# The MLP's last weight, w4, cut into loads in another way

## The chip, the core and the metric

The kernel runs on one core of one Trainium2 chip. The metric is the device time of one execution in microseconds (us), as the median of several runs.

## The reference

One decode step with one token of 512 values. `xn` is the layer norm of `x`. Two branches read it. The first is attention over a cache: 32 heads of 128, and of each head's K and V cache the last 4096 rows are used (32 heads x 4096 x 128 x 2 bytes, 33.5 MB each for K and V). The second is a small MLP with the weights w1 to w4. The result joins the two:

```
q  = xn @ wq                               # 32 heads of 128
s  = softmax(q . k / sqrt(128)) . v @ wo   # last 4096 rows of each head
x1 = xn + hs                               # hs: shifted gelu(ln(xn) @ w1) @ w2; zero for one token
g  = silu(x1 + gelu(ln(x1) @ w3) @ w4)     # w3: 512 x 1376, w4: 1376 x 512
out = x + s * g
```

With one token all four shifted parts of `h` are zeros, so the kernel neither loads w1 nor computes h; it multiplies w2 with zeros.

## The kernel before

The kernel streams K and V once and is otherwise arranged around that stream.

**Loads.** Three small loads go out on ACT: `x_bf`, `x_row` (four rows, one to every 32nd partition) and `wq_sb` (4 MB). All others go out on SP through `load` (L75 to L76): `w2_sb`, `w3_sb`, then w4 in two loads (L91, L92), then the K and V tiles, and the wo rows between and behind them. Ten rows of w4 go to each of 128 partitions (10 KB in one piece: partition p holds rows 10p to 10p+9), and the 96 rows that are left go one to a partition, in the tile's eleventh column. A K or V tile (`load_kv`) is 4 MB for a group of four heads. The first K tile comes in two halves, and so do its computations; the last V tile comes in three pieces. There are three K buffers and two V buffers, so a load waits until the tile that it replaces has been used.

**Order.** In the main part, `tc.manual_schedule` keeps TensorE, VectorE and ScalarE in the order in which the loop over steps `s` writes the work out. Step s loads K of group s and V of group s-2. For each K tile, VectorE computes 64 or 80 of the 128 score columns as products and sums (`k_vector`, L321 and L323); the other columns are transposed on TensorE (`k_turn`, L339), copied by ScalarE (L342) and multiplied with q on TensorE (`k_scores`, L350). The softmax of a group runs a step later, the products with V (`v_wide`, L427) two steps later. V buffers and the last wo rows reuse the memory of the weights (`wts`), so the first V load waits until the MLP is done with them. At the end, `v_part` (L461) uses the last piece of V, `v_out` (L471) divides, `y_head` multiplies the last four heads with wo (L155), and L651 and L653 join the branches and store the result.

**The MLP.** It runs while the stream starts. `a_ps` (L252) takes z3 times w3 as rows: the 1376 values lie in PSUM rows 0, 32, 64 and 96, three blocks of 128 in each. Block i must hold the values that go with the i-th w4 row of every partition, so w3's columns are read with a stride. Gelu (L255), transposes (L258) and a copy (L260) turn them into columns `a_bf`. Then 4 matmuls with w2 and 11 with w4 (L270) add up into `hr_ps`, one for each w4 row of a partition. `hr` (L273) copies the sum, two small steps (L155, L278) bring it into rows, and L280 gives `g_row`, which is used at the very end.

Of the kernel before, what the change touches and what calls it, by code (L numbers as in the profile page):

```python
# [8 lines left out]
P = 128  # L9
BF16 = mybir.dt.bfloat16  # L10
# [16 lines left out]
def kernel(  # L27
# [16 lines left out]
    Bb, Sq, D = A_x.shape  # L44
# [8 lines left out]
    PB = P // G  # L53
    KC = D // P
    F = B_w3.shape[1]
    assert F == 10 * P + 96
    scale = float(Dh) ** -0.5


# [13 lines left out]
    wts = wts_guard.__enter__()  # L73

    def load(dst, src):  # L75
        return tc.keep_in_program_order(nc.sync.dma_start(out=dst, in_=src))  # L76
# [10 lines left out]
    load(w2_sb[:], B_w2.rearrange("(p c) n -> p c n", p=P))  # L87
    w3_sb = wts.tile([P, KC, F], BF16, name="w3_sb")
    load(w3_sb[:], B_w3.rearrange("(p c) n -> p c n", p=P))
    w4_sb = wts.tile([P, 11, D], BF16, name="w4_sb")  # L90
    load(w4_sb[:, 0:10, :], B_w4[0:10 * P, :].rearrange("(p c) n -> p c n", p=P))  # L91
    load(w4_sb[0:96, 10, :], B_w4[10 * P:F, :])  # L92


    def load_kv(pool, cache, g, cuts=(0, CP)):
# [107 lines left out]
    for b in range(2):  # L203
        zeros(qr[b][:])
        for c in range(KC):
            wc = wq_sb[:, c, :].rearrange("p (g a d) -> p g a d", a=G, d=Dh)
# [38 lines left out]
    a_ps = ps_misc.tile([P, 3, P], FP32, tag="misc", name="a_ps")  # L245
    zeros(a_ps[:])
    for c in range(KC):
        wc = w3_sb[:, c, 0:10 * P].rearrange("p (q r) -> p r q", r=10)
        parts = [(j, a_ps[32 * j:32 * j + 1, :, :], wc[:, 3 * j:3 * j + 3, :]) for j in range(3)]
        parts += [(3, a_ps[96:97, 0, :], wc[:, 9, :]), (3, a_ps[96:97, 1, 0:96], w3_sb[:, c, 10 * P:F])]  # L250
        for j, dst, w in parts:
            nc.tensor.matmul(dst, lhsT=z3_bf[:, c:c + 1], rhs=w, start=False, stop=(c == KC - 1),  # L252
                             skip_group_check=True)
# [8 lines left out]
    hr_ps = ps_misc.tile([P, KC, P], FP32, tag="misc", name="hr_ps")  # L262
    zeros(hr_ps[:])
    terms = [(shifted_bf[:, c:c + 1], w2_sb[:, c, :]) for c in range(KC)]
    for i in range(11):
        n = P if i < 10 else 96
        terms.append((a_bf[0:n, i % 3, i // 3:i // 3 + 1], w4_sb[0:n, i, :]))
    for i, (col, w) in enumerate(terms):
        r = 32 * (i % 4)
# [415 lines left out]
```

## Time and profile before

| | before |
|---|---|
| median of 3 runs | 193.7 us (193.29 to 194.14) |
| profiled execution: span | 191.2 us |
| DMA | 79.02 MB, mean 413 GB/s |
| packets | 4572, of these under 2 KB 1232 |
| VectorE busy | 150.9 us (79%) |
| TensorE matmul busy | 116.4 us (61%) |
| ScalarE busy | 89.2 us (47%) |

The span runs from the first to the last instruction of one profiled execution; the timed runs hold some 2.5 us more around it. Busy time is a sum over the whole span. A load's packets are spread over 16 DMA engines. The page gives the engines' mean share; the trace also keeps every packet's start and duration, and, for every load, one increment of its completion semaphore from each DMA engine that took part. A load has landed when the last of them has come.

### The profile page before, as it was taken

The page shows a single profiled execution, that of the slowest core. Times are in us where ns is not written, and L with a number is a line of the kernel's source. Part 1 is how long each engine was busy: PE and PEld are TensorE (multiplying, and loading weights), DVE is VectorE, ACT ScalarE, POOL GpSimd, SP SyncE. Part 2 cuts the span into 40 slices and gives each one's busy share as a digit, 9 for nine tenths or more (in the row PEclk, how much of TensorE's full clock was granted, in tenths as well). Part 3 has the DMA queues.
Part 4 walks back from the last instruction along what each step waited for, and adds up shares of the span by engine and source line. Part 5 has one row for each costly group of instructions (what it writes and reads, how often), then busy time and mean ns, then how long its engine had stood idle before and what let it go on. Part 6 is the DMA issues. An engine that isn't in the chain of part 4 may idle for free.

```text
span 191.2 us, 2839 instructions
## 1 busy us (share of the span) xinstructions
PE 116.4 (61%) x1159; PEld 74.2 (39%) x1159; DVE 150.9 (79%) x175; ACT 89.2 (47%) x191; POOL 2.3 (1%) x11
## 2 busy tenths in 40 slices
PE   1653754989825368256845772680888189739762
PEld 0430222767614334143334441540763077313322
DVE  1660159979999999999999999999999999980111
ACT  2001370888794076427464564542475148733120
POOL 2110000000000000000000000000000000000000
PEclk9999695555755557955695588557567858975998
DMA  6999999999999999999999999999999998999990
GB/s 211 447 430 404 431 418 439 439 439 437 432 434 439 432 429 432 432 439 432 422 432 432 418 422 418 452 439 435 439 432 434 435 432 372 471 425 405 420 371 32
DMA packets 4572, 79.02 MB, mean 413 GB/s; under 512 B 624, under 2 KB 1232, under 8 KB 1488
## 3 DMA queue, kind: packets, MB, share of 16 engines
q1 hardware_dynamic: 4264, 74.65, 91.6%
q10 hardware_dynamic: 296, 4.20, 5.1%
q8 instruction: 9, 0.15, 0.3%
q14 instruction: 3, 0.02, 0.0%
HBM read 78.84 MB, written 0.00 MB: 412 GB/s over the span
## 4 chain that ended last, share of the span: by engine, by line
DVE 46%; DMA 43%; PE 5%; ACT 3%; issue 1%; SPq 1%; ACTq 0%; DVEq 0%
DMA kv<-in_A_k_cache_dram 31%; DVE S L323 28%; DVE prod L321 15%; DMA kv<-in_A_v_cache_dram 10%; ACT kt L342 3%; DMA x_bf<-in_A_x_dram 2%; PE pt L339 2%; PE ov L427 1%; DVE m L366 1%; DVE S L364 1%; SPq L76 1%; PE sT L350 1%; DVE mx L374 1%; PE oT L461 1%; PE ot_ps L444 0%
## 5 line engine op out<-in xcount | busy, mean ns | idle before, releaser
L323 DVE TENSOR_REDUCE S<-prod 128x20 f32<-128x2560 bf16 (+1 forms) x32 | 86.0, 2686 | 1.1
L342 ACT COPY kt<-pt 128x1024 bf16<-128x1024 bf16 x52 | 51.2, 1013 | 40.4 <-PE pt L339 38.7
L339 PE MATMUL pt<-ident_f,kv 128*128 128x128 f32 x208 | 46.7, 376 | 10.8 <-DMA kv<-in_A_k_cache_dram 10.8
L321 DVE TENSOR_TENSOR prod<-kv,q_bc 128x2560 bf16<-128x2560 bf16 (+1 forms) x32 | 45.4, 1418 | 3.9 <-DMA kv<-in_A_k_cache_dram 3.7
L339 PEld LDWEIGHTS pt<-ident_f,kv 128*128 128x128 f32 x208 | 34.2, 196 | 14.4 <-DMA kv<-in_A_k_cache_dram 10.5
L350 PE MATMUL sT<-q_pair,kt 128*128 128x8 bf16 x416 | 19.4, 170 | 15.7 <-ACT kt L342 15.5
L350 PEld LDWEIGHTS <-kt 128*128 128x128 bf16 x416 | 16.4, 104 | 26.8 <-ACT kt L342 25.8
L427 PE MATMUL ov<-kv,pT 128*16 128x512 bf16 x248 | 22.0, 515 | 1.4 <-DMA kv<-in_A_v_cache_dram 1.4
L388 ACT ACTIVATE pT<-S,mb 128x128 bf16<-128x128 f32 x32 | 13.9, 573 | 0.3
L372 PE MATMUL mt_ps<-ident_f,m 128*1 128x128 f32 x8 | 2.9, 359 | 17.4 <-DVE rden L399 16.9
L433 ACT COPY ov_sb<-ov 128x512 f32<-128x512 f32 x8 | 4.7, 586 | 17.1 <-PE ov L427 17.1
L427 PEld LDWEIGHTS <-pT 128*16 128x16 bf16 x248 | 6.9, 109 | 13.2 <-issue 11.4
L359 ACT ACTIVATE own<-sT,par 128x48 f32<-128x48 f32 (+1 forms) x32 | 7.5, 356 | 3.7 <-PE sT L350 3.7
L444 PE MATMUL ot_ps<-ident_f,ov_sb 128*128 128x128 f32 x32 | 7.1, 359 | 2.9 <-ACT mb L384 1.9
L211 DVE CAST q_row<-qr_ps 128x512 bf16<-128x512 f32 x1 | 0.7, 692 | 9.9 <-PE qr_ps L208 9.9
L388 ACT ACTIVATION_READ_ACCUMULATOR pT<-S,mb 128x1 f32 x32 | 8.3, 258 | 0.0
L372 PEld LDWEIGHTS mt_ps<-ident_f,m 128*1 128x1 f32 x8 | 0.6, 80 | 17.9 <-DVE rden L399 17.2
L399 DVE RECIPROCAL rden<-den_ps 128x4 f32<-128x4 f32 x8 | 1.4, 175 | 7.0 <-PE den_ps L394 7.0
L381 PE MATMUL mb_ps<-md,par_t 5*128 5x4 f32 x16 | 3.9, 311 | 4.1 <-DVE md L376 4.1
L255 ACT ACTIVATE a_row<-a_ps 128x384 bf16<-128x384 f32 x1 | 0.5, 491 | 12.0 <-remote 12.0
L444 PEld LDWEIGHTS ot_ps<-ident_f,ov_sb 128*128 128x128 f32 x32 | 4.5, 178 | 3.9 <-ACT mb L384 2.3
L208 PE MATMUL qr_ps<-wq_sb,xq_bf 128*1 128x512 bf16 x32 | 3.1, 566 | 3.7 <-DMA wq_sb<-in_A_wq_dram 3.7
(122 smaller groups left out, 81.6 us busy)
## 6 DMA issues: line engine op xcount, KB each, us to landing
kv<-in_A_k_cache_dram SPq DMA_DIRECT2D x7, 4096.0 KB, 31.3
kv<-in_A_v_cache_dram SPq DMA_DIRECT2D x7, 4096.0 KB, 30.6
wq_sb<-in_A_wq_dram ACTq DMA_DIRECT2D x1, 4096.0 KB, 17.6
kv<-in_A_k_cache_dram SPq DMA_DIRECT2D x2, 2048.0 KB, 27.4
wo<-in_A_wo_dram SPq DMA_DIRECT2D x1, 2048.0 KB
kv<-in_A_v_cache_dram SPq DMA_DIRECT2D x1, 2048.0 KB
kv<-in_A_v_cache_dram SPq DMA_DIRECT2D x2, 1024.0 KB, 17.6
w_sb<-in_B_w_dram SPq DMA_DIRECT2D x1, 1376.0 KB, 9.1
```

The source lines that it names most:

```text
L321: nc.vector.tensor_tensor(out=prod[:, 0:m, :], in0=kn[:, rows, :], in1=q_bc[:, g:g + 1, :].to_broadcast([P, m, Dh]), op=ALU.mult)
L323: nc.vector.tensor_reduce(out=st[g]["S"][:, rows], in_=prod[:, 0:m, :], axis=AX.X, op=ALU.add)
L339: nc.tensor.transpose(pt[:, i, :], kn[:, c:c + 2, :].rearrange("p c d -> p (c d)").bitcast(FP32), ident_f[:])
L342: nc.scalar.copy(out=kts[b][:, 0:n, :], in_=pt[:, 0:n, :].bitcast(BF16))
L350: nc.tensor.matmul(st[g]["sT"][:, c:c + 2, :].rearrange("p c a -> p (c a)"), lhsT=kt[:, i, l::2], rhs=q_pair[:, g, l, :], start=(l == 0), ...
L359: nc.scalar.mul(s["own"][:, 0:m, a], s["sT"][:, 0:m, a], par[:, a:a + 1])
L372: nc.tensor.transpose(mt_ps[:], s["m1"][:], ident_f[:])
L381: nc.tensor.matmul(mb_ps[:], lhsT=par_t[:].rearrange("k b a -> k (b a)"), rhs=md[:], start=True, stop=True)
L388: nc.scalar.activation(out=s["pT"][:, :, a], in_=s["S"][:], func=ACT.Exp, scale=scale, bias=mb[:, a:a + 1], accum_out=s["sum"][:, a:a + 1])
L427: nc.tensor.matmul(ov[r:r + 4 * G], lhsT=s["pT"][:, c:c + 4, :].rearrange("p i a -> p (i a)"), rhs=v[:, c:c + 4, :], start=(i < 4), stop=( ...
L433: nc.scalar.copy(out=s["ov_sb"][:], in_=ov[:])
L444: nc.tensor.transpose(ot_ps[:, step * j:step * j + P], s["ov_sb"][:, j, :], ident_f[:])
```

## The change

w4's 1376 rows are cut as 9 x 128 + 216 + 8 instead of 10 x 128 + 96. Nine rows go to each partition. The next 216 rows are cut into 72 pieces of three rows (3 KB each), which go to 72 partitions in columns 9 to 11; the source is written as six runs of twelve pieces (`e = lanes`). Eight rows of 1 KB go to partitions 72 to 79 in column 9. SP issues three loads for w4 where it issued two. The a_ps matmuls follow: for each of the four c there are three wide ones, three of 72 columns and one of 8, where there were three wide ones, one of 128 and one of 96. hr_ps has 12 products with w4 instead of 11: nine with 128 rows, one with 80 and two with 72. The tile w4_sb has 12 columns instead of 11.

```
-    w4_sb = wts.tile([P, 11, D], BF16, name="w4_sb")
-    load(w4_sb[:, 0:10, :], B_w4[0:10 * P, :].rearrange("(p c) n -> p c n", p=P))
-    load(w4_sb[0:96, 10, :], B_w4[10 * P:F, :])
+    w4_sb = wts.tile([P, 12, D], BF16, name="w4_sb")
+    few, lanes = 72, 6
+    f_few, f_rest = 9 * P, 9 * P + 3 * few
+    load(w4_sb[:, 0:9, :], B_w4[0:f_few, :].rearrange("(p c) n -> p c n", p=P))
+    load(w4_sb[0:few, 9:12, :].rearrange("p c n -> p (c n)"),
+         B_w4[f_few:f_rest, :].rearrange("(i e c) n -> e i (c n)", e=lanes, c=3))
+    load(w4_sb[few:few + F - f_rest, 9, :], B_w4[f_rest:F, :])
...
-        wc = w3_sb[:, c, 0:10 * P].rearrange("p (q r) -> p r q", r=10)
+        wc = w3_sb[:, c, 0:f_few].rearrange("p (q r) -> p r q", r=9)
         parts = [(j, a_ps[32 * j:32 * j + 1, :, :], wc[:, 3 * j:3 * j + 3, :]) for j in range(3)]
-        parts += [(3, a_ps[96:97, 0, :], wc[:, 9, :]), (3, a_ps[96:97, 1, 0:96], w3_sb[:, c, 10 * P:F])]
+        wf = w3_sb[:, c, f_few:f_rest].rearrange("p (i e r) -> p r e i", e=lanes, r=3)
+        parts += [(3, a_ps[96:97, r, 0:few].rearrange("o (e i) -> o e i", e=lanes), wf[:, r]) for r in range(3)]
+        parts += [(3, a_ps[96:97, 0, few:few + F - f_rest], w3_sb[:, c, f_rest:F])]
...
-    for i in range(11):
-        n = P if i < 10 else 96
+    for i in range(12):
+        n = P if i < 9 else few + F - f_rest if i == 9 else few
```

More of the change, by code (lines that the diff above doesn't have):

```diff
@@ L55 @@
     F = B_w3.shape[1]
-    assert F == 10 * P + 96
+    assert F == 9 * P + 3 * 6 * 12 + 8
     scale = float(Dh) ** -0.5
```

## The prediction

> **What bounds the kernel now.** I read the page's DMA rows first, then the chain of waits, then the time around w4, then the trace's records of single packets.
>
> Page, second and third parts (busy share in 40 slices, GB/s, then queue: packets, MB, share of 16 engines' span):
>
> ```profile
> DMA  6999999999999999999999999999999998999990
> ...
> q1 hardware_dynamic: 4264, 74.65, 91.6%
> ...
> q8 instruction: 9, 0.15, 0.3%
> q14 instruction: 3, 0.02, 0.0%
> ```
>
> The DMA engines are full from the second slice to the last but one. Two small queues, q8 and q14, fetch instructions in between.
>
> Chain of waits, its last part (start us, us, what):
>
> ```profile
> 130.25 23.26 DMA kv<-in_A_k_cache_dram
> ...
> 167.79 18.54 DMA kv<-in_A_v_cache_dram
> 186.33 0.05 issue
> 186.38 0.97 PE oT L461 x32
> 187.35 0.02 issue
> 187.37 0.17 DVE o L471
> 187.55 0.04 issue
> 187.59 0.42 PE y_ps L155 x16
> ```
>
> The last piece of V lands at 186.33; the 4.85 us behind it are fixed. Before it DVE is the chain from 41.9 to 130.2, but the K load that DVE lets go at 130.25 lands 23 us later, behind others in the queue, where a 4 MB load takes 9.7 us (79 MB at 413 GB/s over the span). So the end is the DMA stream's end. As every load is queued well ahead, each of the 16 DMA engines runs through its own list without gaps, and **the end is that of the last engine**, not the mean.
>
> The trace keeps one increment for each engine and load. The last V load's 16 increments fall at 184.31, .31, .33, .38, .55, .61 and then 185.46, .78, .90, .93, .99, 186.00, .04, .11, .24, .33. Six engines are ready 1.3 to 2.0 us before the rest. The reason can be followed: in the packet records every packet of an engine begins 3 to 4 ns before the one ahead of it ends, so each engine's row of packets can be strung together from 2.5 us to the end. Eight engines carry one q8 fetch each (27.7, 47.2, 69.1, 91.7, 111.2, 130.7, 150.0 and 175.3 us; each costs its engine about 1.55 us), two carry the three q14 fetches (0.7 to 1.0 us each at 47.1 and 54.3), six carry none. Those two are the 185.46 and the 185.78.
>
> **The change, part by part.** Packet times (queue row, size): 1 KB 46 ns, 4 KB 159, 8 KB 309, 10 KB 385, all less the 4 ns of overlap.
>
> *Nine rows instead of ten.* 128 packets, 8 to an engine, of 9 KB: between 309 and 385, so 347. Each engine saves 8 x 38 = 0.30 us.
>
> *96 rows of 1 KB go.* Six packets and an increment to an engine, 6 x 42.6 + 6 = 0.26 us saved on each. Both together: 0.57 us off every engine.
>
> *216 rows in 72 packets of 3 KB, in six runs.* 12 packets to an engine, if six engines take them. 3 KB is not in the trace: at most three 1 KB packets (138 ns), at least three quarters of a 4 KB one (119); I take 121, on the line through both. 12 x 117 + 6 = 1.41 us (1.39 to 1.62) on each of six engines, nothing on ten. *Eight rows of 1 KB*: 0.05 us on eight engines.
>
> Sums: the six gain 1.41 + 0.05 - 0.57 = **+0.89 us** (to 1.10); the other ten get 0.52 to 0.57 us shorter. The bytes are the same.
>
> *Which six* decides. The row that bears on it is x_row, a load of four rows: it shows four increments where 128-row loads show 16, so a load of six runs on six is credible. x_row's four packets (5.41, 5.44, 5.47, 5.99 us) can be followed to the end on their engines: two are clean, one comes out as the 185.46 and one as the 185.78 (the two q14 engines). At two places a partner with the same phase could be swapped in, but those partners are q8 engines, later still. I take it that a load of six runs takes in the engines that a load of four does, plus two clean ones. Then the 185.78 becomes 186.67, the 185.46 becomes 186.35, the clean ones at most 185.50; the eight q8 engines end at 185.76. The last increment moves from 186.33 to 186.67: **+0.34 us**.
>
> [...]
>
> *One load more on SP.* Five w loads instead of four, 0.42 us of SP each. More important, the built program shows the loads' eight completion semaphores going round, each load waiting for the landing of the load eight before. So the K loads' waits move by one: the first half of K0 now waits for x_bf, the second for w2, K1 for x_row, K2 for wq. The page's waits (us, times, longest) show what these are:
>
> ```profile
> SPq L76 <- DMA wq_sb<-in_A_wq_dram: 12.5, 1, 12.5
> ...
> SPq L76 <- DMA x_bf<-in_A_x_dram: 1.4, 1, 1.4
> SPq L76 <- DMA x_row<-in_A_x_dram: 0.9, 1, 0.9
> ```
>
> K0 goes out at 4.7 instead of 2.6 us, but its first packet starts at 20.04, behind w4. K2 goes out when wq has landed (19.9) instead of 6.8 us; K1's packets keep the queue full until 40. V0, next on SP, waits for hr until 31.2 us anyhow. Cost nothing; if that cover were gone, 2 us for K0.
>
> *TensorE and the first products.* Timeline:
>
> ```profile
> 13.25 2.92 PE L252 MATMUL a_ps<-w_sb,z_bf 128*1 128x384 bf16 x20 [0.77 <-DVE md L303]
> ...
> 25.60 0.82 PE L270 MATMUL hr_ps<-w_sb,a_bf 128*1 128x512 bf16 x11
> 26.09 1.23 DVE L321 TENSOR_TENSOR prod<-kv,q_bc 128x2048 bf16<-128x2048 bf16 x1 [2.19 <-DMA kv<-in_A_k_cache_dram]
> ```
>
> 28 a_ps matmuls instead of 20 over the same 1376 columns: 8 more, at 0.15 us (2.92/20) some 1.2 us (0 to 2), in front of a 3.7 us wait of TensorE for wq. One hr_ps matmul more (0.07 us; 0.38 alone), and DVE fetches hr only at 29.55. w4 lands near 22 instead of 21.2, used at 25.6. K0's first half lands 0.7 to 0.9 us later on the six engines, so DVE's first product starts near 26.8; DVE then idles 0.99 us before K1's first product at 41.9 (K1's last increment, a q8 engine's, comes 0.57 earlier), which takes it up. If it did not, K7's load would be issued 0.9 us later, still ahead of 13 us of queue. [...]
>
> **Sum.** Span 191.2 + 0.34 = 191.5. The profiled span lies 2.5 us under the median of the runs, 193.7, and nothing in the change touches what lies around it: **194.0 us**.
>
> **Rivals.**
>
> *A. The six are the six clean engines.* Then 184.61 becomes 185.50 and the late ones 185.76: -0.57 us, **193.1**. For it: the clean engines are just six. Against: x_row's engines, two of which are not clean. [...]
>
> *B. The six hold a q8 engine* (slower). The price is +0.89 on an engine that ends between 185.90 and 186.33, so the end moves by +0.46 to +0.89: **194.2 to 194.6**. It decides from one such engine on. For it: x_row says only where four of the six are; the swaps named above. Against: q8 seems to go round just eight engines (the ninth fetch begins as the first one's engine ends), none of them x_row's.
>
> *C. The load doesn't stay on six*: spread over 16, 12 x 117 x 6/16 = 0.53 us against 0.57 saved: no change, **193.7**.
>
> **How the numbers follow.** Forecast 0.45, A 0.20, B 0.25, C 0.10. A difference of 0.5% (1.0 us, from 192.7 to 194.7) is about what a measurement of this kernel can tell from no change. All four cases lie inside it; outside come only B with its upper packet price (194.8), and A or the run-to-run spread (193.3 to 194.1 over three runs) on top. So faster 0.05, same 0.80, slower 0.15. Range 193.0 to 194.7: it takes in A, C and B's dearest case at the packet price taken.
>
> **What would show it.** In the profile after: 1 KB rows fewer by 88 and 72 packets of 3 KB at 121 ns; the last V load's increments with one or two engines alone at the end, 0.3 us later (forecast), six more early ones gone (A), or a cluster near 187 (B); K0's first product near 26.8; a K2 wait on wq of 12 to 13 us; no DMA slice under 9 that was 9 before. I would be wrong if the stream showed a gap near 40 us, or if fetches fell on other engines than before.

## The result, and the profile after

The changed kernel takes 194.93 us (median of 6 runs, 194.79 to 195.34) against 193.53 us (193.29 to 194.14) for the kernel before beside it: ratio 1.0074, 95% interval 1.0061 to 1.0088. It is 1.40 us slower, where 0.3 us was forecast, and outside the range.

The span of the profiled execution is 192.6 us. The page's DMA rows of the changed kernel, which answer to those shown of before (busy share and GB/s in 40 slices of 4.8 us, then packets, MB, share of the queues):

```profile
DMA  6998999999999999999999999999999999999980
GB/s 207 460 466 358 367 425 435 435 435 427 435 430 435 432 435 435 435 435 435 432 435 435 425 435 391 480 425 429 429 429 430 418 435 394 457 435 412 413 331 8
...
q1 hardware_dynamic: 4246, 74.65, 91.2%
...
q8 instruction: 9, 0.15, 0.3%
q14 instruction: 3, 0.02, 0.0%
```

The second line for the kernel before, of which the prediction shows the first:

```profile
GB/s 211 447 430 404 431 418 439 439 439 437 432 434 439 432 429 432 432 439 432 422 432 432 418 422 418 452 439 435 439 432 434 435 432 372 471 425 405 420 371 32
```

The bytes and the fetches are the same, the DMA engines stay full. The fourth slice's 8 is no gap: the third and the fourth together moved 466 and 358 GB/s, before 430 and 404, so the mean of the two is 412 against 417. The fifth slice matters: 367 GB/s where the kernel before moved 431. The loss is in there, as the time in stretches around the w4 loads shows (columns: stretch, us, busy us of PE, PEld, DVE, ACT, POOL, TensorE's granted clock, DMA share, GB/s). Before:

```profile
20.20:22.20 2.00, 2.00 (x24) 0.69 (x20) 0.00 (x0) 0.36 (x1) 0.00 (x0) 0.50 1.09 450
```

After:

```profile
19.00:20.20 1.20, 0.53 (x8) 0.24 (x11) 0.00 (x0) 0.00 (x0) 0.00 (x0) 0.50 1.03 413
20.20:22.20 2.00, 2.00 (x28) 0.57 (x20) 0.00 (x0) 0.59 (x1) 0.00 (x0) 0.50 1.04 285
22.20:24.00 1.80, 1.80 (x16) 0.62 (x9) 0.69 (x1) 0.79 (x2) 0.00 (x0) 0.50 1.01 428
```

For two microseconds the DMA engines are just as busy (share 1.04) and move 285 GB/s instead of 450. These are the microseconds in which the 72 packets of 3 KB are in flight, from 19.6 to 21.6; their load shows six increments, at 22.11 to 22.52. The packet records say how: packets of 3 KB take 121 to 344 ns (35 of the 72 take 121), and the 16 KB packets of K0 beside them up to 1125 ns where nearly all others of that size take 611. Summed over the packets that start between 19 and 24 us, the time above the usual duration of their size is 12.5 us, in the kernel before 1.2. This sum is called **the excess** from here on; divided by 16 engines, the difference is 0.7 us an engine.

The chain of waits ends as before, with the last piece of V, which lands at 187.63 instead of 186.33 (17.01 us after 170.62):

```profile
170.62 17.01 DMA kv<-in_A_v_cache_dram
```

Behind it nothing has changed: from the landing to the last output store it is 2.35 us in both. The 16 increments of that piece fall at 184.43, .64, .84, then ten from 185.89 to 186.25, and three alone at 187.03, 187.41, 187.63. Another load is close behind: the last rows of wo land at 187.61 in the kernel before and at 188.96 in the changed one, 0.09 and 0.05 us ahead of the matmul that waits for them.

### The profile page after: what moved, and what is told of

Its sections match the earlier page's. It is cut to its first block, busy times and chain, and to the rows that moved or that the text cites. A ratio compares the mean times of both kernels' runs of the same rounds, so it can differ in the third digit from the quotient of the medians.

```text
span 192.6 us, 2858 instructions
## 1 busy us (share of the span) xinstructions
PE 120.1 (62%) x1168; PEld 76.0 (39%) x1168; DVE 151.1 (78%) x175; ACT 89.3 (46%) x191; POOL 2.3 (1%) x11
## 4 chain that ended last, share of the span: by engine, by line
DVE 55%; DMA 35%; PE 6%; issue 1%; ACT 1%; SPq 0%; DVEq 0%; ACTq 0%
DVE S L329 33%; DMA kv<-in_A_k_cache_dram 24%; DVE prod L327 17%; DMA kv<-in_A_v_cache_dram 9%; PE ov L433 3%; DMA x_bf<-in_A_x_dram 2%; ACT kt L348 1%; DVE m L372 1%; DVE S L370 1%; PE pt L345 1%; PE ot_ps L450 1%; DVE mx L380 1%; PE oT L467 1%; PE mb_ps L387 0%; SPq L76 0%
## 5 line engine op out<-in xcount | busy, mean ns | idle before, releaser
L345 PE MATMUL pt<-ident_f,kv 128*128 128x128 f32 x208 | 46.2, 373 | 9.9 <-DMA kv<-in_A_k_cache_dram 9.9
L356 PE MATMUL sT<-q_pair,kt 128*128 128x8 bf16 x416 | 19.4, 170 | 15.9 <-ACT kt L348 15.8
L433 PE MATMUL ov<-kv,pT 128*16 128x512 bf16 x248 | 24.1, 555 | 0.5 <-DMA kv<-in_A_v_cache_dram 0.4
L212 PE MATMUL qr_ps<-wq_sb,xq_bf 128*1 128x512 bf16 x32 | 3.6, 626 | 3.5 <-DMA wq_sb<-in_A_wq_dram 3.5
```

Source lines behind the costliest of these rows:

```text
L212: nc.tensor.matmul(qr[b][32 * a:32 * a + 1], lhsT=xq_bf[:, c:c + 1], rhs=wc[:, 4 * b:4 * b + 4, a, :], start=False, stop=(c == KC - 1), sk ...
L345: nc.tensor.transpose(pt[:, i, :], kn[:, c:c + 2, :].rearrange("p c d -> p (c d)").bitcast(FP32), ident_f[:])
L356: nc.tensor.matmul(st[g]["sT"][:, c:c + 2, :].rearrange("p c a -> p (c a)"), lhsT=kt[:, i, l::2], rhs=q_pair[:, g, l, :], start=(l == 0), ...
L433: nc.tensor.matmul(ov[r:r + 4 * G], lhsT=s["pT"][:, c:c + 4, :].rearrange("p i a -> p (i a)"), rhs=v[:, c:c + 4, :], start=(i < 4), stop=( ...
```

## The experiments

Two things stood against each other after the comparison. **The uneven split** (theory 1 in the texts below): the six carry 1.4 us more each, and one of them is an engine with a q8 fetch (rival B), so the end moves. **The slowdown** (theory 2): something in the change makes all packets beside it slow for 2 us. The slowdown itself could come from the shifted order of waits (K loads go out at other times), from the load of six as such, from the order of its source, from the size of its pieces, or from the partitions that it writes to.

**The shifted waits alone.** The kernel before with its 96 rows in two loads, so that the K loads wait for other semaphores:

```
-    load(w4_sb[0:96, 10, :], B_w4[10 * P:F, :])
+    load(w4_sb[0:80, 10, :], B_w4[10 * P:10 * P + 80, :])
+    load(w4_sb[80:96, 10, :], B_w4[10 * P + 80:F, :])
```

> The kernel before with its 96 rows cut into 80 and 16 (all 16 engines in both): one more load on SP, so K2's load is issued at about 19.7 us as in the changed kernel, but no engine carries more than before. Theory 1 (the load of six runs lengthens engines that are late anyhow): no change, within 0.1 us of before (193.5). Theory 2a (the stretch of 285 GB/s between 20.2 and 22.2 us is due to K2's load being issued just before it): the stretch shows here too and the time is up by 0.7 us (194.2). Theory 2b (the stretch is due to the six-run load's packets beside K's): no such stretch, no change.

Measured: 193.58 us, ratio 1.0008 (0.9998 to 1.0018), 442 GB/s from 20.2 to 22.2 us, excess 1.5 us. The waits cost nothing, as the prediction had it, and theory 2a is out. K2 waits for wq here as in the changed kernel: SP's first four K loads take 15.68 us from 4.83, where they take 4.77 us from 2.59 in the kernel before.

**Twelve runs, sixteen runs.** The changed kernel with other splits of the same rows; in the second, 64 pieces of three rows and 32 rows of 1 KB.

```
-    few, lanes = 72, 6
+    few, lanes = 72, 12      # first
+    few, lanes = 64, 16      # second
```

> The changed kernel with twelve runs of six pieces instead of six runs of twelve. Theory 1: twelve engines gain 6 x 117 ns + 6 - 570 = +0.14 us (+0.19 with a 1 KB row), four are 0.57 us shorter: +0.2 us over before (193.7). Theory 2a: +0.9 us (194.4), with the slow stretch as long as in the changed kernel. Theory 2b: the pieces are in flight for half as long, so a slow stretch of about 1 us and +0.5 us (194.0).

> 64 pieces of three rows in sixteen runs and 32 rows of 1 KB, so that all 16 engines carry the same; packets as large as in the change. Theory 1: 4 x 117 + 6 + 2 x 42.6 + 6 - 570 = 0.00 us on each engine: as before, 193.5. Theory 2a: +0.7 us (194.2). Theory 2b: the pieces are in flight for a third of the time, about +0.2 us (193.7).

Measured: twelve 194.18 us, ratio 1.0031 (1.0018 to 1.0043), 420 GB/s, excess 4.3 us; sixteen 193.97 us, ratio 1.0024 (1.0014 to 1.0033), 401 GB/s, excess 4.7 us. The last V increments come at 186.44 and 186.63, with nobody alone at the end. Both times are 0.2 to 0.3 us above what theory 2b gave. So an even split takes about half of the loss away or somewhat more, but not all: with sixteen runs every engine is meant to have the same bytes, none is alone at the end, and it is still slower than before, with an excess three to four times that of before. The slowdown is not a matter of six engines alone.

**The load of six earlier.** The changed kernel with the same load moved up in the program, while w3 and wq stream. It stands behind w2's load (the expectation says ahead of w2's, which the edit does not do):

```
     load(w2_sb[:], B_w2.rearrange("(p c) n -> p c n", p=P))
+    w4_sb = wts.tile([P, 12, D], BF16, name="w4_sb")
+    load(w4_sb[0:few, 9:12, :].rearrange("p c n -> p (c n)"),
+         B_w4[f_few:f_rest, :].rearrange("(i e c) n -> e i (c n)", e=lanes, c=3))
     w3_sb = wts.tile([P, KC, F], BF16, name="w3_sb")
...
```

> The changed kernel with the six-run load as the first of SP's loads, ahead of w2, so that its packets lie beside w2's and x's and no longer beside K's. Theory 1 alone: the six engines carry as much as in the change; where one of them is a late one, +0.5 to +0.9 us over before (194.0 to 194.4). Theory 2a: the slow stretch at 20.2 us stays, 194.9 as the changed kernel. Theory 2b: the stretch goes from 20.2 us; if it needs K's packets beside it the time falls to 194.0 to 194.4, if the load slows whatever lies beside it, it shows at 2 to 5 us instead and the time stays near 194.9.

Measured: 195.64 us, ratio 1.0107 (1.0092 to 1.0122). The time in stretches, this kernel:

```profile
1.00:4.50 3.50, 0.60 (x1) 0.09 (x1) 0.34 (x5) 1.28 (x1) 0.77 (x4) 1.00 0.74 182
4.50:8.00 3.50, 1.74 (x21) 1.59 (x21) 1.46 (x9) 0.00 (x0) 0.35 (x1) 1.00 0.93 320
20.20:22.20 2.00, 1.72 (x25) 1.40 (x28) 0.00 (x0) 0.00 (x0) 0.00 (x0) 1.00 1.06 450
```

The kernel before in the first two:

```profile
1.00:4.50 3.50, 0.59 (x1) 0.09 (x1) 0.34 (x5) 1.28 (x1) 0.76 (x4) 1.00 0.81 248
4.50:8.00 3.50, 1.90 (x21) 1.63 (x21) 1.47 (x9) 0.00 (x0) 0.50 (x1) 1.00 1.02 427
```

The slow stretch goes where the load goes, and w4's old place is back at 450. In the new place some of w3's packets, of 413 ns, are among the victims: twelve of the 128 take 514 to 2267, while 70 of the six's own 72 pieces keep to 121. So the load slowed w3's packets here as it slowed K0's there. That the kernel is 0.7 us slower than the changed one, where 194.9 was expected, is not explained by this. In its profiled execution the last V load lands at 188.43, and the last products with wo start 1.99 us behind it instead of 1.26: TensorE is late there, and the stream is not all that ends the kernel. In the profiled execution of the shifted waits, the longest of its twelve, it is the same (2.04 us).

**Probes.** To change one thing at a time, the kernel before got one extra load of the same 216 KB into a tile that nothing reads, behind the w4 loads. They were run once each, beside runs of the kernel before of 193.38 us (one run, for the first four) and 193.46 us (median of 16, from 193.12 to 194.19). A single time can thus be off by most of 1 us; the packets of each profile carry the argument. The kernel before in the stretch that is compared:

```profile
20.50:22.50 2.00, 2.00 (x28) 0.62 (x20) 0.00 (x0) 0.62 (x2) 0.00 (x0) 0.50 0.98 410
```

First the source: as in the change (each of the six runs takes every sixth piece), and as six stretches of 36 rows, 37 rows apart, one for each run.

```
+    probe = wts.tile([P, 1536], BF16, name="probe")
+    load(probe[0:72, :],
+         B_w4[9 * P:9 * P + 216, :].rearrange("r n -> (r n)").rearrange("(i e m) -> e i m", e=6, m=1536))
```

> The kernel before with the 216-row load of six runs added behind its w4 loads, into a tile that nothing reads (72 partitions x 3 KB); 0.22 MB more is read than the reference needs. It takes the load out of the change, for comparison with the next three. All theories of the slow stretch expect it here as in the changed kernel: near 285 GB/s between 20.5 and 22.5 us, the packets together some 11 us over their usual durations.

> As p0, but each of the six engines reads one run of 36 KB (runs 37 rows apart) instead of every sixth piece of 3 KB. Source theory (six engines reading interleaved pieces of one small stretch of memory slow all reads): the stretch goes, under 3 us over. Target theory (pieces written to partitions that other engines are writing to): as p0, some 11 us over.

Measured: as in the change 195.43 us, excess 13.9; one run of rows 195.63 us, excess 14.5. Time in stretches of the first (in the second 312 GB/s):

```profile
20.50:22.50 2.00, 2.00 (x25) 0.64 (x20) 0.00 (x0) 0.63 (x2) 0.00 (x0) 0.50 1.18 327
```

The probe reproduces the slowdown, and the order of the source is innocent. Next, the same bytes as 48 pieces of 4.5 KB in partitions 0 to 47 (each run eight neighbours), and as 24 pieces of 9 KB in partitions 0 to 23 (each run four: run e of the six, counted from 0, writes 4e to 4e+3). The second is shown; the first has 48 partitions and m=2304.

```
+    probe = wts.tile([P, 4608], BF16, name="probe")
+    load(probe[0:24, :],
+         B_w4[9 * P:9 * P + 216, :].rearrange("r n -> (r n)").rearrange("(i e m) -> e i m", e=6, m=4608))
```

> As p0 with 8 pieces of 4.5 KB to an engine on 48 partitions, source interleaved as in p0. Target theory, if an engine's share of a 128-partition load is eight neighbouring partitions: each of the six then writes to its own partitions and the stretch goes, under 3 us over; if its share lies otherwise, near 11 us. Source theory: as p0, some 11 us over.

> As p0 with 4 pieces of 9 KB to an engine on 24 partitions. Target theory, if an engine's share of a 128-partition load begins with four neighbouring partitions and its other four lie elsewhere: no stretch, under 3 us over; with eight neighbours as in p2's case, over 5 us. Source theory: still interleaved, 5 to 11 us over.

Measured: 48 partitions 196.21 us, 263 GB/s, excess 19.4 (4.5 KB taken at 178 ns, the least that is seen); 24 partitions 194.48 us, excess 0.1. The same stretch of the kernel with 24:

```profile
20.50:22.50 2.00, 2.00 (x24) 0.68 (x20) 0.00 (x0) 0.68 (x2) 0.00 (x0) 0.50 1.05 447
```

With eight neighbours to a run the slowdown is there, with four it is gone. (Of the 196.21 us some 0.5 are not the stream's: the last products with wo start 1.81 us behind V there, not 1.26.) But two things differ in the last probe, the partitions and the size of the pieces. So the same 24 pieces were moved down the partitions, by 24 and by 32:

```
-    load(probe[0:24, :],
+    load(probe[24:48, :],     # first
+    load(probe[32:56, :],     # second
```

> The kernel before with an extra load of 216 rows as 24 pieces of 9 KB on six engines, as in the probe with partitions 0 to 23, but written to partitions 24 to 47; nothing reads it. Only the partitions differ, so size and number of the pieces are the same. Theory (what slows all packets is that an engine writes to partitions which another engine writes in the loads of 128 rows): slow again, 280 to 340 GB/s from 20.5 to 22.5 us, 12 to 20 us of packet time above the usual durations, and 195.4 to 196.2 us. Rival (few large pieces are harmless, many small ones are not, wherever they go): as the probe with partitions 0 to 23, some 447 GB/s, under 1 us above the usual, 194.5 us.

> The same load of 24 pieces of 9 KB, written to partitions 32 to 55. In a load of 128 rows an engine has 8 packets, so it writes eight partitions, of which the probes so far show four (4e to 4e+3 for engine e). If the other four are elsewhere, this probe is as slow as the one with partitions 24 to 47: 280 to 340 GB/s, 12 to 20 us above the usual, 195.4 to 196.2 us. If partitions 32 lower share a way into the memory, no slowdown: about 447 GB/s, under 1 us, 194.5 us. [...]

Measured: by 24, 195.87 us, excess 21.9; by 32, 194.74 us, excess 0.0. The same stretch, partitions 24 to 47:

```profile
20.50:22.50 2.00, 2.00 (x24) 0.64 (x20) 0.00 (x0) 0.65 (x2) 0.00 (x0) 0.50 1.05 226
```

Partitions 32 to 55:

```profile
20.50:22.50 2.00, 2.00 (x28) 0.60 (x16) 0.00 (x0) 1.15 (x2) 0.00 (x0) 0.51 1.07 455
```

With nothing changed but the place, half the rate (226 GB/s) or none lost (455). **It is the partitions**: the load of six runs is harmless where run e writes 4e to 4e+3 (excess 0.1 us) or 32 above that (0.0), and slow where it writes 24 above (21.9). With the move by 24 a 9 KB packet takes 700 ns in the median instead of 347, and the slowest 16 KB packets 1314 instead of 611: about twice. The three probes agree with the theory of the expectation, that what counts is whether an engine writes partitions which another engine writes in the large loads. Its mechanism is not shown: the trace has no engine numbers and no partitions, so which engine writes which of them, in this load and in the large ones, is the author's reading of the three excesses, and so are the "own four" partitions of an engine in the expectations. That some partitions are slow whoever writes them does not fit: the harmless probes leave out only 24 to 31 of the partitions from 24 to 47, eight pieces, and 13 of the 24 take 682 ns or more. The split in sixteen (excess 4.7 us) fits the theory: its 64 pieces, four to a run in order, put those of the runs 8 to 15 into partitions 32 to 63, of which in the probe the runs 0 to 5 wrote 32 to 55 without harm; this was not tested by itself.

**The change without the slowdown.** The changed kernel, with the 216 rows as 24 pieces of nine rows in partitions 0 to 23, again in six runs:

```
-    w4_sb = wts.tile([P, 12, D], BF16, name="w4_sb")
-    few, lanes = 72, 6
-    f_few, f_rest = 9 * P, 9 * P + 3 * few
+    w4_sb = wts.tile([P, 18, D], BF16, name="w4_sb")
+    few, lanes = 24, 6
+    f_few, f_rest = 9 * P, 9 * P + 9 * few
...
-    load(w4_sb[0:few, 9:12, :].rearrange("p c n -> p (c n)"),
-         B_w4[f_few:f_rest, :].rearrange("(i e c) n -> e i (c n)", e=lanes, c=3))
+    load(w4_sb[0:few, 9:18, :].rearrange("p c n -> p (c n)"),
+         B_w4[f_few:f_rest, :].rearrange("(i e c) n -> e i (c n)", e=lanes, c=9))
...
-        wf = w3_sb[:, c, f_few:f_rest].rearrange("p (i e r) -> p r e i", e=lanes, r=3)
+        wf = w3_sb[:, c, f_few:f_rest].rearrange("p (i e r) -> p r e i", e=lanes, r=9)
```

> The changed kernel with the 216 rows as 24 pieces of nine rows (9 KB) on the same six engines, in partitions 0 to 23, where each engine stays in its own four; nine rows and eight rows as in the changed kernel. Of the nine rows in each of these partitions only three enter the product (the other 144 rows are left out of it), so the sums of the MLP are not the reference's. Theory (the changed kernel loses by two things, a slowdown of all packets of 0.7 to 0.8 us an engine and one late engine among the six): without the slowdown only the late engine is left. The probe with these pieces added 1.38 us on each of the six; less 0.56 for the tenth row and the 96 rows, and 0.05 for the eight rows, the six gain 0.87 and the last increment goes from 186.33 to 186.7 to 187.2, so 193.9 to 194.3 us, ratio to before 1.002 to 1.005; from 20 to 22 us no slice below 430 GB/s. Rival (it is all the uneven split over engines): as the changed kernel, 194.9 us, ratio 1.007. Rival (it is all the slowdown): 193.4 us, ratio 1.000.

Measured: 194.17 us, ratio 1.0035 (1.0022 to 1.0047), excess 0.0. The time in stretches:

```profile
19.00:20.20 1.20, 0.42 (x8) 0.19 (x11) 0.00 (x0) 0.00 (x0) 0.00 (x0) 1.00 1.04 438
20.20:22.20 2.00, 2.00 (x28) 0.62 (x20) 0.00 (x0) 1.10 (x2) 0.00 (x0) 0.57 0.98 419
22.20:24.00 1.80, 1.80 (x14) 0.78 (x7) 0.86 (x2) 0.80 (x3) 0.00 (x0) 0.53 1.02 437
```

No slow stretch (419 stands between 438 and 437: a little under the 430 that was expected, with no packet above its usual time). Half of the loss is left, between the two rivals, as the theory of two causes said.

The end of the stream takes it apart. The last V load's three late increments are at 186.23, 186.44 and 186.71 in this kernel, at 187.03, 187.41 and 187.63 in the changed one, and 186.33 was the last before. So in these executions, one of each kernel, the uneven split costs 0.38 us and the slowdown 0.92, together the 1.30 by which the stream ends later. The slowdown reaches all 16 engines: the increments of K0's first half, right behind it, are ten at 25.05 to 25.33 and six at 26.29 to 26.48 here, ten at 25.69 to 26.09 and six at 27.13 to 27.31 in the changed kernel.

The 0.71 us of the medians is more than 0.38. In the profiled execution 0.21 of it lies behind the stream: the last 16 matmuls with wo ran at a granted clock of 0.50 and took 0.60 us, in the kernel before at 1.00 and 0.39. First before, then this kernel:

```profile
187.59 0.39 PE L155 MATMUL y_ps<-wo_rows,o 128*1 128x128 bf16 x16 [0.26 <-DVE o L471]
```

```profile
187.97 0.60 PE L159 MATMUL y_ps<-wo_rows,o 128*1 128x128 bf16 x16 [0.26 <-DVE o L477]
```

That leaves 0.1 us unexplained. In the changed kernel these matmuls take 0.39, in four of the other experiments 0.59 or 0.60, at a clock of 0.50 there too. Whether the clock of the tail belongs to a kernel or to an execution was not measured.

**Two engines instead of six.** Could a version win by giving only early engines more? The kernel before with 80 of its 96 rows as eight pieces of 10 KB in a load of two runs (taken to be two engines, as the load of six runs shows six increments), in partitions 0 to 7:

```
-    w4_sb = wts.tile([P, 11, D], BF16, name="w4_sb")
+    w4_sb = wts.tile([P, 20, D], BF16, name="w4_sb")
...
-    load(w4_sb[0:96, 10, :], B_w4[10 * P:F, :])
+    load(w4_sb[0:8, 10:20, :].rearrange("p c n -> p (c n)"),
+         B_w4[10 * P:10 * P + 80, :].rearrange("(i e c) n -> e i (c n)", e=2, c=10))
+    load(w4_sb[8:24, 10, :], B_w4[10 * P + 80:F, :])
...
-        n = P if i < 10 else 96
+        n = P if i < 10 else 24
```

> The kernel before with its 96 rows as eight pieces of ten rows (10 KB) by a load of two runs, in partitions 0 to 7, and 16 rows of 1 KB in partitions 8 to 23; ten rows to a partition as before. Of the 80 rows of the eight pieces only eight enter the product (72 rows are left out of it), so the sums of the MLP are not the reference's. All engines lose 0.22 to 0.26 us, two gain 4 times 0.381 + 0.006 = 1.53 us. If both are engines without instruction fetches (184.3 to 184.6 before), they end near 185.9 and the rest at 186.1 at most: time 193.2 to 193.4 us, ratio 0.998 to 1.000, at the limit of what can be told. If one of them carries fetches (185.46 or 185.78 before) it ends at 186.75 to 187.1: 193.8 to 194.2 us, ratio 1.002 to 1.004. No slow stretch in either case.

Measured: 194.29 us, ratio 1.0041 (1.0027 to 1.0055), excess 0.0, the last V increments five from 183.88 to 184.32, ten from 184.98 to 185.85 and one at 187.04. (With fetches on one of the two engines, 193.8 to 194.2 us was expected, and its end at 186.75 to 187.1.) One of the six early engines has left its group, so it is one of the two; the other is an engine with fetches, and ends 1.2 us behind all others. The rest end 0.4 to 0.5 us earlier than before, 0.2 more than was expected and not explained, and the one engine takes it all back. No version here beats the kernel before.

## Why the prediction was wrong, point by point

**The bound** was right for the two kernels: the end is the last DMA engine's, the increments say which, and what lies behind is unchanged. Three of its numbers are off, and nothing rests on them. Of the three q14 fetches the last falls at 147.1 us. A tile of 4096 KB takes 10.2 us at 413 GB/s, not 9.7. The 2.5 us around the span compare two different executions; where the record has both for one, they lie 2.2 us apart (194.79 and 192.6 us, for the changed kernel).

**"12 x 117 + 6 = 1.41 us (1.39 to 1.62) on each of six engines, nothing on ten"**: the step that failed is "nothing on ten". A load was priced as packets by the duration of a packet of its size, on its own engines. Where its packets went was not in the price, and for 2 us the engines together moved 285 GB/s instead of 450. Price: 0.7 to 1.0 us on each of the 16 at the end of the last V load, 0.92 on the last of them. By the medians that is half of the loss (0.71 of 1.40 us are left without the slowdown), by the end of the stream 0.92 of 1.30. It was neither in the sum nor in a rival, and the range could not hold it. The price on the six alone was nearly right: the first half of K0 parts by 1.2 us (without the slowdown) to 1.4 us (with it) between the six and the ten, where 0.89 + 0.57 = 1.46 was the forecast.

**Nine rows and no 96 rows, -0.57 us** held. Without the slowdown, the three engines that carry no fetch and nothing of the six's load end at 183.69 to 184.08, where the six earliest before ended at 184.31 to 184.61.

**Which six**: half right. In the probe with 24 partitions each engine's packets can again be strung together, with some swaps left open. The four engines of x_row are all among the six, as taken. "Plus two clean ones" was wrong: one is clean, the other is a q8 engine (its fetch at 91.98 us), which is what rival B names. The counts at the end agree: without the slowdown three increments come late and three early, as when three of the six carry fetches and three engines have neither a fetch nor a part of the load. By this reading the two q14 engines come at 186.23 and 186.44 without the slowdown (forecast 186.35 and 186.67), the q8 engine is the 186.71. That the sum of the forecast, 186.67, lies so near is chance: it was read from another engine. B asked for 0.46 to 0.89, from 186.79 up; the end moved by 0.38, a little under its lower edge.

**One load more on SP** was right. K2's wait for wq is there, 12 to 13 us as foretold, and costs nothing, as the experiment with the shifted waits shows. The row of the waits alone can't show it, as the kernel before has one of 12.5 us too; that it now stands before K2 shows in SP's first four K loads. The row of the changed kernel, then SP's timeline before and after:

```profile
SPq L76 <- DMA wq_sb<-in_A_wq_dram: 12.7, 1, 12.7
```

```profile
2.59 4.77 SPq L76 DMA_DIRECT2D kv<-in_A_k_cache_dram  x4
```

```profile
4.63 15.55 SPq L76 DMA_DIRECT2D kv<-in_A_k_cache_dram  x4
```

**TensorE and the first products**: the eight more a_ps matmuls cost 0.1 us instead of 1.2 (20 took 2.92, the 28 take 3.02). The first product starts later than 26.8, by the same 0.6 to 0.9 that the slowdown takes from K0:

```profile
13.17 3.02 PE L258 MATMUL a_ps<-w_sb,z_bf 128*1 128x384 bf16 x28 [0.78 <-DVE md L309]
...
27.41 1.23 DVE L327 TENSOR_TENSOR prod<-kv,q_bc 128x2048 bf16<-128x2048 bf16 x1 [3.09 <-DMA kv<-in_A_k_cache_dram]
```

Most of the delay of 1.32 us is taken up before K1, as foretold, but it is more than the 0.99 that DVE had to spare: K1's first product begins at 42.27 instead of 41.91, with no wait for K1 ahead of it. The DMA engines stay full all the same.

**What would show it**: packets of 3 KB at 121 ns came true for 35 of the 72. "One or two engines alone at the end" were three, and higher. Fetches fell on as many places as before, nine and three.

## What to carry to other kernels

A load on fewer than 16 engines need not be paid for by its own engines alone: here one on six cost each of the 16 between 0.7 and 1.0 us. Look where it writes: the same 24 pieces of 9 KB cost no packet time in partitions 0 to 23 and 32 to 55 (excess 0.1 and 0.0 us) and 21.9 us of it in 24 to 47. Try such a load in another place, and look for a stretch with the DMA engines as busy as ever and GB/s low (here 1.04 and 285, where it was 1.09 and 450). And in a stream that has no gaps, extra bytes belong on engines that end early, which has to be known engine by engine, not guessed from four of six.

## What the runs showed of the hardware

- Place: in the probes' loads of six runs (216 KB), packets whose run e wrote partitions 4e to 4e+3, or 32 above that, kept their usual time (excess 0.1 and 0.0 us). With 24 above, and with eight or twelve neighbours to a run, many did not, nor did packets beside them (13.9 to 21.9 us). All 16 engines lost by it (with the move by 24, the 16 last increments came 1.3 to 1.6 us later than without, all of them); that was not expected, and its way is not settled by these runs.
- Even the 96 rows of 1 KB in the kernel before seem to do a little of it to K0's packets right behind them (argued from the excess, not tested): the 1.2 us there are 0.0 in the two kernels without such a load and with harmless pieces, and 0.0 and 0.1 in the two probes where harmless packets stand between them and K0.
- Packet time, without disturbance, is on one line from 1 to 32 KB: 46 ns for 1 KB, 121 for 3, 347 for 9, 611 for 16, 1213 for 32.
- The end of the kernel moves by 0.2 us with the clock granted to the last 16 matmuls (0.39 at 1.00, 0.60 at 0.50).
